# ScalarE issues the stores of h; the weights of the next expert are issued at the head of an item

## The chip, the cores and the metric

The kernel runs on one core of one Trainium2 chip. The metric is the device time of one execution in microseconds. Five engines work side by side: TensorE (PE; its weight loads are shown as PEld), VectorE (DVE), ScalarE (ACT), GpSimd (POOL) and SyncE (SP), which here only issues transfers and reads registers. Each engine works through its own instructions in order. A transfer is issued by one instruction and moved by 16 DMA engines. The three timed runs before the change took 784.21, 784.96 and 787.46 us; the median is 784.96 us.

## What is computed

Local attention with 32 global tokens for 8 batches of 8 heads (512 local queries, window 32, head size 64), then a mixture of experts over the 4352 resulting rows of 512. Each row goes to the one expert of eight with the largest logit:

```
for e in range(E):
    mask = expert_idx == e
    h = np.maximum(x[mask] @ w1[e], 0.0)
    out[mask] = gate_w[mask, None] * (h @ w2[e])
```

w1[e] is 512 x 1024 and w2[e] is 1024 x 512, all in float32. The change touches the second part only.

## The kernel before, in words

The attention part ends by scattering its rows, sorted by expert, into the DRAM tensor `xs`. The expert part then works on *items*: blocks of 128 rows that belong to one expert. 32 items always run; the rest, up to 48, stand in nested branches on the number of items (`rest`), and 36 run here. `item(w, pend)` writes one item's instructions; the order in it is the order on every engine, since it is written under a manual schedule.

Precision: a float32 product is made of three products in a faster form of float32. Each operand is split into a high part (a cast on ScalarE: `WH`, `xH`, `hH`) and a low part (operand less high part, on VectorE or GpSimd: `WL`, `xL`, `hL`). TensorE then sums high x high, high x low and low x high.

An item's path: its rows `xr` and gates `gt` come from `xs` (`load_x`, issued two items ahead: four transfers and one for gt). `up(0)` and `up(1)` are the two halves of x @ w1, twelve products each, into PSUM `g`. `relu` writes half of `h`. The half is then stored to DRAM (`put_h`, tile `hd`) and read back (`get_h`, tile `hq`), which does part of its transposition; VectorE turns it within blocks (`turn_h`, tile `hk`), and `split_h` makes hH and hL. In the item after, `down(0)` and `down(1)` are the two halves of h @ w2, and in the one after that `give` scales the result by the gate (line 173) and scatters it to the output. So TensorE's order in item w is up(0), up(1) of w, then down(0), down(1) of w-1.

Weights: an expert's 4096 x 2 columns per partition come through two stages, `st0[0]` and `st0[1]` (tile `stg`), one an item by turns. `load_w(w + 1)` fills the stage of the next item in two transfers of 1024 KB, each carried out only where a table says so; of one expert's four, most items carry out one or none. Every item casts its stage in eight parts, `w_part(0)` to `w_part(7)`: WH on ScalarE (line 1284), WL on VectorE, parts 0 and 4 on GpSimd (line 1286). They belong to the next expert, so no product of this item reads them. The parts of the first expert's weights (`first_parts`, line 1207 and 1209) are made from the stages before the first item.

Before the change, SP issues within item w: put_h 0, load_x(w + 2), get_h 0, put_h 1, load_w(w + 1), get_h 1. Each put_h waits for its relu. Register reads for the addresses and conditions (line 1217) stand ahead of load_x and load_w on SP. ScalarE's order is: line 173, parts 0 and 1, hH of the first half, parts 2 and 3, relu 0, parts 4 and 5, relu 1, hH of the second half, parts 6 and 7, xH of the next item.

Transfers issued by SP and ScalarE take turns at eight completion semaphores, shown as DMAHW0 to DMAHW7 in the order below; the next transfer of a lane waits until the one before it has landed.

Of the kernel before, what the change touches and what calls it, by code (L numbers as in the profile page):

```python
# [94 lines left out]
def _max_items(nt):  # L95
    return (nt - (NE - 1)) // P + 1 + 2 * (NE - 1)
# [11 lines left out]
def tile_kernel(ctx: ExitStack, tc: tile.TileContext, qk, va, emb, tau, wraw, cst, out):  # L108
    nc = tc.nc
# [3 lines left out]
    NI = _max_items(NT)  # L113
# [30 lines left out]
    def cols(st, lo, hi):  # L144

        r = lo // WRUN
        return st[:, r, lo - r * WRUN : hi - r * WRUN]
# [3 lines left out]
    def rows_of(x, gt, rows, turned=False):  # L151

        made = []
        for g in range(4):
            src = rows[:, g * P : (g + 1) * P].rearrange("(t i) n -> i t n", t=4)
            made.append(nc.sync.dma_start(x[32 * g : 32 * g + 32].rearrange("p (t n) -> p t n", n=P), src))
        src = rows[:, DM:ROW]
        made.append(nc.sync.dma_start(gt, src.rearrange("(i t) n -> t i n", t=4) if turned else src))
        return made
# [5 lines left out]
    def turn_blocks(xT, x):  # L165

        nc.vector.transpose(  # L167
            xT.rearrange("p (k t n) -> p t k n", k=4, t=4), x.rearrange("p (t k n) -> p t k n", t=4, k=4)
        )
# [99 lines left out]
    with ExitStack() as actx:  # L269
# [40 lines left out]
        parts = []  # L310
# [593 lines left out]
        for b in range(NB):  # L904
# [4 lines left out]
            for part in range(3):  # L909
                g = 4 * b + (2 + part // 2 if b else 4)  # L910
# [81 lines left out]
        for g in loads:  # L992
            n = len(loads[g])
# [209 lines left out]
    def first_parts(hf, c):  # L1203

        cs = slice(c * 1024, (c + 1) * 1024)
        src = cols(st0[hf], cs.start, cs.stop)
        nc.scalar.copy(WH[:, hf, cs], src)
        eng = nc.gpsimd if hf == 1 and c < 2 else nc.vector
        eng.tensor_tensor(WL[:, hf, cs], src, WH[:, hf, cs], ALU.subtract)
# [3 lines left out]
    def entry(eng, i, w, top):  # L1213

        if w < 2:
            return (EARLY * P + w * P, 2 + w, 0, 2 + w)[i]
        return eng.value_load(tab["tab"][w : w + 1, i : i + 1], min_val=0, max_val=top)

    def load_x(w):
        r = entry(nc.sync, 0, w, NE * CAP)  # L1220
        return rows_of(xrs[w % 2], gts[w % 5], xs[ds(r, P), :], True)

    def load_w(w):
        r = entry(nc.sync, 1, w, 2 * NE - 1)
        src = wraw[ds(r, 1), :, :].rearrange("a p (c n) -> p (a c) n", n=WRUN)
        for n in range(2):
            cs = slice(2 * n, 2 * n + 2)
            new = {} if w < 2 else {"cond": entry(nc.sync, 4 + n, w, 1)}
            nc.sync.dma_start(st0[w % 2][:, cs, :WRUN], src[:, cs, :], **new)

    def parts_of(tH, tL, x):
        nc.scalar.copy(tH, x)  # L1232
        nc.vector.tensor_tensor(tL, x, tH, ALU.subtract)  # L1233

    def flat(t):
        return t.rearrange("p c n -> p (c n)")
# [5 lines left out]
    def split_x(w):  # L1242
        parts_of(flat(xHs[w % 2]), flat(xLs[w % 2]), xk)
# [4 lines left out]
    hs = [h[:, :DM], h[:, DM:]]  # L1248

    def relu(nh, g):  # L1250
        nc.scalar.activation(
            hs[nh].rearrange("p (g k n) -> p k g n", g=4, k=4),
            g.rearrange("p (k g n) -> p k g n", k=4, g=4),
            AF.Relu,
        )

    def put_h(w, nh):
        hd = hds[w % 2][nh].rearrange("p n -> (p n)").rearrange("(g p n) -> p g n", g=4, p=P)
        nc.sync.dma_start(hd, hs[nh].rearrange("p (g n) -> p g n", g=4))

    def get_h(w, nh):
        nc.sync.dma_start(hqs[nh], hds[w % 2][nh])

    def turn_h(nh):
        turn_blocks(hk, hqs[nh])

    def split_h(nh):
        ks = slice(4 * nh, 4 * nh + 4)
        parts_of(flat(hH[:, ks, :]), flat(hL[:, ks, :]), hk)

    def item(w, pend):

        st, xH, xL = st0[w % 2], xHs[w % 2], xLs[w % 2]
        rp = entry(nc.tensor, 2, w, 1)
        ra = entry(nc.scalar, 3, w, 3)
        rv = entry(nc.vector, 3, w, 3)
        rg = entry(nc.gpsimd, 3, w, 3)
        reads = []
        made = []

        def w_part(c):
            cs = slice(c * 512, (c + 1) * 512)
            s3 = cols(st, cs.start, cs.stop).unsqueeze(1)
            made.append(nc.scalar.copy(WH[:, ds(ra, 1), cs], s3))  # L1284
            eng, r = (nc.gpsimd, rg) if c % 4 == 0 else (nc.vector, rv)
            made.append(eng.tensor_tensor(WL[:, ds(r, 1), cs], s3, WH[:, ds(r, 1), cs], ALU.subtract))  # L1286

        def product(o, a, W, col, start=False, stop=False):
            return nc.tensor.matmul(o.unsqueeze(1), a, W[:, ds(rp, 1), col : col + 512], start=start, stop=stop)  # L1289

        def up(nh):
            g = ps_1.tile([P, 512], F32, name="g1")
            for k in range(4):
                col = k * 1024 + nh * 512
                reads.append(product(g, xH[:, k, :], WH2, col, start=k == 0))
                reads.append(product(g, xH[:, k, :], WL2, col))
                reads.append(product(g, xL[:, k, :], WH2, col, stop=k == 3))
            return g

        out = {}  # L1300

        def down(nh):
            if nh == 0:
                out["g2"] = g2s[w % 2]
            g, ks, made = out["g2"], range(4 * nh, 4 * nh + 4), []
            for k in ks:
                made.append(product(g, hH[:, k, :], WH2, 4096 + k * 512, start=k == 0))
                made.append(product(g, hH[:, k, :], WL2, 4096 + k * 512))
            for k in ks:
                made.append(product(g, hL[:, k, :], WH2, 4096 + k * 512, stop=k == 7))  # L1310
            return made

        def done():
            give(gts[w % 5], out["g2"], obp.tile([P, DM + 1], F32, name="ob"))

        late = "down" in pend
        ga = up(0)
        if "done" in pend:
            pend["done"]()
        w_part(0)  # L1320
        if late:
            turn_h(0)
        w_part(1)
        if late:
            split_h(0)
        w_part(2)
        w_part(3)
        relu(0, ga)
        put_h(w, 0)
        if w + 2 < NI:  # L1330
            load_x(w + 2)
        gb = up(1)
        w_part(4)
        if late:
            turn_h(1)
        w_part(5)
        if late:
            reads.extend(pend["down"](0))
        relu(1, gb)
        get_h(w, 0)  # L1340
        put_h(w, 1)
        if w + 1 < NI:
            load_w(w + 1)
        if late:
            split_h(1)
        w_part(6)
        if 0 < w < NI - 1:
            turn_blocks(xk, xrs[(w + 1) % 2])
        w_part(7)
        if 0 < w < NI - 1:  # L1350
            split_x(w + 1)
        get_h(w, 1)
        if w in (8, NSURE - 1):
            nc.gpsimd.drain()
        if late:
            reads.extend(pend["down"](1))
        for m in made:
            for r in reads:
                tc.declare_no_dep(m.ins, r.ins, reason="the other slot")
                tc.declare_no_dep(r.ins, m.ins, reason="the other slot")  # L1360
            for o in last_made:
                if o.ins.engine != m.ins.engine:
                    tc.declare_no_dep(m.ins, o.ins, reason="another half")
        for i, m in enumerate(made):
            for o in made[: i // 2 * 2]:
                if o.ins.engine != m.ins.engine:
                    tc.declare_no_dep(m.ins, o.ins, reason="other columns")
        last_made[:] = made
        after = {"down": down, "next": done}
        if "next" in pend:  # L1370
            after["done"] = pend["next"]
        return after
# [10 lines left out]
    with tc.manual_schedule():  # L1383
        nc.vector.tensor_copy(runi, run[:1])
        for e in range(NE):
            fill_rest(e)
        load_x(0)
        load_x(1)
        tab["tab"], nitem = table()
        parts = [(hf, c) for hf in range(2) for c in range(4)]  # L1390
        for i, f in enumerate(block):
            if i == 9:
                x_parts(0)
            if i:
                f()
            for _ in range((3, 0, 1, 0, 0, 1, 0, 1, 0, 0, 0)[i]):
                first_parts(*parts.pop(0))
        x_parts(1)
        for hf, c in parts:
            first_parts(hf, c)  # L1400
        load_w(0)
        pend = {}
        for w in range(NSURE):
            pend = item(w, pend)
# [94 lines left out]
```

## Time and profile before

| | |
|---|---|
| median of three runs | 784.96 us (784.21 to 787.46) |
| the profiled execution | 784.63 us, span 782.80 us |
| mean granted clock of TensorE | 0.944 of full speed |
| busy over the span | PE 669.3, DVE 545.3, ACT 464.3, POOL 201.2 us |

The span runs from the first to the last instruction; the execution's own time is longer by what lies around it. Busy time is an average over parts with different limits: an engine that is busy 85% of the span can be idle in one place and the limit in another. So the trace is read by stretches and by waits. Register reads, waits and the issuing of transfers do not count as busy. "x2" in a line of the timeline means two instructions merged into one row, whose time is their sum; brackets show how long the engine sat idle before the row and what ended that. The row of a transfer on SPq is the time of its issue alone, not of the movement.

### The profile page before, as it was taken

How to read it: one execution, taken by the hardware profiler on the slowest of the kernel's cores; microseconds unless marked ns; L12 is line 12 of the kernel's file. 1: busy time of each engine (PE TensorE's matmuls, PEld its weight loads, DVE VectorE, ACT ScalarE, POOL GpSimd, SP SyncE). 2: the span in 40 equal slices, each digit the busy share in tenths (PEclk: the TensorE clock that was granted, in tenths of full speed). 3: DMA queues.
4: the chain of work that ended last, by engine and by line, in shares of the span. 5: the costliest groups of instructions: out<-in, count | busy, mean ns of one | idle time of the engine just before them, and what ended most of it. 6: DMA issues, size and time to landing. Idle time of an engine off the chain costs nothing. (4 is left out here: it accounts for less than half of the span.)

```text
span 782.8 us, 23722 instructions
## 1 busy us (share of the span) xinstructions
PE 669.3 (85%) x7425; PEld 505.0 (65%) x7425; DVE 545.3 (70%) x1642; ACT 464.3 (59%) x954; POOL 201.2 (26%) x246
## 2 busy tenths in 40 slices
PE   9888878798889967789999888968988878789994
PEld 4666666676665446567777666757666656567773
DVE  2667877887776755568889567657468666577892
ACT  4666776577672445557766456545456555566661
POOL 2001222222223522213333222322222222223231
PEclk9899999999998988889999999998999999989997
DMA  8888987888991874566545556556556567565441
GB/s 255 292 264 244 274 272 236 276 272 264 305 279 61 231 258 147 149 180 183 145 127 145 164 172 209 169 189 186 164 170 195 163 208 219 156 185 175 127 135 61
DMA packets 125596, 154.70 MB, mean 198 GB/s; under 512 B 15881, under 2 KB 81545, under 8 KB 125464
## 3 DMA queue, kind: packets, MB, share of 16 engines
q1 hardware_dynamic: 119704, 135.20, 58.3%
q0 software_dynamic: 5760, 17.87, 6.1%
q8 instruction: 68, 1.11, 0.6%
q14 instruction: 64, 0.52, 0.2%
HBM read 161.36 MB, written 40.94 MB: 258 GB/s over the span
## 5 line engine op out<-in xcount | busy, mean ns | idle before, releaser
L1286 DVE TENSOR_TENSOR WL<-stg,WH 128x512 f32 (+1 forms) x216 | 209.8, 973 | 104.8 <-ACT WH L1284 96.6
L1284 ACT CAST WH<-stg 128x512 f32 (+1 forms) x288 | 177.0, 618 | 113.6 <-DMA stg<-in_wraw_dram 109.0
L1289 PE MATMUL g<-WH,hH 128*128 (+1 forms) x288 | 127.6, 443 | 67.3 <-ACT hH L1232 67.1
L1286 POOL TENSOR_TENSOR WL<-stg,WH 128x512 f32 (+1 forms) x72 | 102.8, 1428 | 155.0 <-ACT WH L1284 128.3
L1289 PE MATMUL g<-WL,hH 128*128 (+1 forms) x288 | 123.4, 428 | 0.0
L1289 PEld LDWEIGHTS g<-WH,hH 128*128 128x128 f32 x288 | 59.6, 207 | 96.7 <-ACT hH L1232 79.8
L1289 PE MATMUL g<-WH,xH 128*128 (+1 forms) x288 | 114.2, 397 | 0.5 <-PE g L1289 0.5
L1289 PE MATMUL g<-WH,xL 128*128 (+1 forms) x288 | 114.2, 397 | 0.0
L1289 PE MATMUL g<-WL,xH 128*128 (+1 forms) x288 | 112.5, 391 | 0.0
L175 POOL DMA_INDIRECT out_dram<-ob x37 | 36.9, 997 | 210.7 <-DVE hk L167 81.5
L552 ACT ACTIVATE pb<-pb,nm 128x128 f32<-128x128 f32 x256 | 80.0, 395 | 12.6 <-DVE nm L535 12.1
L1289 PE MATMUL g<-WH,hL 128*128 (+1 forms) x288 | 82.8, 412 | 0.0
L167 DVE STREAM_TRANSPOSE hk<-hq 128x512 f32<-128x512 f32 x72 | 50.8, 705 | 30.7 <-DMA hq<-hd 30.7
L1289 PEld LDWEIGHTS g<-WH,hL 128*128 128x128 f32 x288 | 59.6, 207 | 13.8
L1289 PEld LDWEIGHTS g<-WL,hH 128*128 128x128 f32 x288 | 60.2, 209 | 12.2
L1289 PEld LDWEIGHTS g<-WH,xL 128*128 128x128 f32 x288 | 54.0, 188 | 16.1 <-DVE xL L1233 5.2
L1289 PEld LDWEIGHTS g<-WH,xH 128*128 128x128 f32 x288 | 54.1, 188 | 15.6 <-ACT xH L1232 5.3
L1289 PEld LDWEIGHTS g<-WL,xH 128*128 128x128 f32 x288 | 54.0, 188 | 11.8 <-DVE xk L167 0.2
L1232 ACT CAST hH<-hk 128x512 fp32r<-128x512 f32 x72 | 44.4, 616 | 26.5 <-DVE hk L167 25.0
L195 PE MATMUL s_ps<-raw 64*32 64x128 f32 (+1 forms) x1792 | 47.9, 284 | 11.0 <-issue 7.1
L195 PE MATMUL po<-vt,pT 128*32 128x65 f32 x2048 | 46.1, 231 | 12.2 <-issue 9.9
L837 POOL DMA_INDIRECT xs<-xt,si x32 | 32.6, 1019 | 76.6 <-PE s_ps L195 27.7
(201 smaller groups left out, 921.6 us busy)
## 6 DMA issues: line engine op xcount, KB each, us to landing
stg<-in_wraw_dram SPq DMA_DIRECT2D x74, 1024.0 KB
vt<-in_va_dram SPq DMA_DIRECT2D x96, 260.0 KB
hd<-h SPq DMA_DIRECT2D x72, 256.0 KB
hq<-hd SPq DMA_DIRECT2D x72, 256.0 KB
raw<-in_qk_dram SPq DMA_DIRECT2D x56, 304.0 KB
xr<-xs SPq DMA_DIRECT2D x152, 64.0 KB
vt<-in_va_dram SPq DMA_DIRECT2D x32, 130.0 KB
stg<-in_wraw_dram SPq DMA_DIRECT2D x16, 256.0 KB
```

The source lines that it names most:

```text
L167: nc.vector.transpose(xT.rearrange("p (k t n) -> p t k n", k=4, t=4), x.rearrange("p (t k n) -> p t k n", t=4, k=4))
L175: nc.gpsimd.indirect_dma_start(out=out[:, :], out_offset=bass.IndirectOffsetOnAxis(ap=ob[:, DM : DM + 1].bitcast(U32), axis=0), in_=ob[:, ...
L195: return counted(nc.tensor.matmul(out, lhsT, rhs, start=start, stop=stop), 4 if lhsT.dtype == F32 else 2)
L552: nc.scalar.activation(pb[:, cs], pb[:, cs], AF.Exp, bias=nm[:, n : n + 1], scale=-1.0)
L837: ins = nc.gpsimd.indirect_dma_start(out=xs[:, :], out_offset=bass.IndirectOffsetOnAxis(ap=st["si"][:, t : t + 1], axis=0), in_=get(t), in ...
L1232: nc.scalar.copy(tH, x)
L1284: made.append(nc.scalar.copy(WH[:, ds(ra, 1), cs], s3))
L1286: made.append(eng.tensor_tensor(WL[:, ds(r, 1), cs], s3, WH[:, ds(r, 1), cs], ALU.subtract))
L1289: return nc.tensor.matmul(o.unsqueeze(1), a, W[:, ds(rp, 1), col : col + 512], start=start, stop=stop)
```

## The change

put_h is issued by ScalarE, right behind its relu. In an item, load_w(w + 1) and load_x(w + 2) are issued first, the weights ahead of x, and both ahead of relu and put_h. Parts 3, 4 and 5 stand between the two relus. In the first item, which has no pending down product, relu and store come first, and the casts of w2's four parts, load_w(1) and all w_parts come behind them.

```diff
     def put_h(w, nh):
-        nc.sync.dma_start(hd, hs[nh].rearrange("p (g n) -> p g n", g=4))
+        nc.scalar.dma_start(hd, hs[nh].rearrange("p (g n) -> p g n", g=4))
...
         if "done" in pend:
             pend["done"]()
-        w_part(0)
+        if w and w + 1 < NI:
+            load_w(w + 1)
+        if w + 2 < NI:
+            load_x(w + 2)
         if late:
+            w_part(0)
             turn_h(0)
-        w_part(1)
-        if late:
+            w_part(1)
             split_h(0)
-        w_part(2)
-        w_part(3)
+            w_part(2)
         relu(0, ga)
         put_h(w, 0)
-        if w + 2 < NI:
-            load_x(w + 2)
         gb = up(1)
-        w_part(4)
         if late:
+            w_part(3)
+            w_part(4)
             turn_h(1)
-        w_part(5)
-        if late:
+            w_part(5)
             reads.extend(pend["down"](0))
+        else:
+            for _ in range(2):
+                first_parts(*parts.pop(0))
         relu(1, gb)
         get_h(w, 0)
         put_h(w, 1)
-        if w + 1 < NI:
-            load_w(w + 1)
         if late:
             split_h(1)
+        else:
+            while parts:
+                first_parts(*parts.pop(0))
+            load_w(w + 1)
+            for c in range(6):
+                w_part(c)
         w_part(6)
...
-            for _ in range((3, 0, 1, 0, 0, 1, 0, 1, 0, 0, 0)[i]):
+            for _ in range((3, 0, 1, 0, 0, 0, 0, 0, 0, 0, 0)[i]):
                 first_parts(*parts.pop(0))
         x_parts(1)
-        for hf, c in parts:
-            first_parts(hf, c)
```

On SP, from the second store of item 2 on, before (hd01 and hd00 are the halves of h in DRAM, stg0 and stg1 the stages; TENSOR_LOAD and ISA read and set registers):

```order
L1259 DMA hd01_59<-h_5768 128x4x128 [waits DMAHW5_49,Activation_49]
L1217 TENSOR_LOAD tab_5920
L1217 ISA x2
L1217 TENSOR_LOAD tab_5920
L1217 ISA x2
L1229 ISA
L1229 DMA stg1_90<-in_wraw_dram 128x2x1024 [waits Pool_49]
L1217 TENSOR_LOAD tab_5920
L1217 ISA x2
L1229 ISA
L1229 DMA stg1_90<-in_wraw_dram 128x2x1024 [waits DMAHW7_49,Pool_49]
L1262 DMA hq_5758<-hd01_59 128x512 [waits DMAHW5_49,DMAHW0_49,DVE_49]
```

The load of the weights for item 3 stands behind both stores of item 2, which wait for ScalarE, and ahead of the second read of h. On SP after the change, from the last transfer of x in item 3 on:

```order
L156 DMA xr1_5751<-xs_57 32x4x128 [waits DMAHW0_49]
L158 ISA
L158 DMA gt0_5752<-xs_57 128x1x2 [waits DMAHW1_49]
L1262 DMA hq_5758<-hd10_60 128x512 [waits DMAHW2_49,DVE_49]
L1262 DMA hq_5758<-hd11_61 128x512 [waits DMAHW4_49,DMAHW3_49,DVE_49]
L1217 TENSOR_LOAD tab_5920
L1217 ISA x2
L1217 TENSOR_LOAD tab_5920
L1217 ISA x2
L1229 ISA
L1229 DMA stg1_90<-in_wraw_dram 128x2x1024 [waits Activation_49,Pool_49]
```

The stores are gone from SP. The load behind the reads of item 3 is now item 4's own, for item 5, and no instruction of item 4 stands ahead of it. The waits on DMAHW1 and DMAHW3 are, by the count of transfers, those on the lanes of the two transfers of item 3's own load of weights.

On ScalarE within one item with a pending down product, before, from the first cast of hH to the second (h<-g is a relu, WH<-stg a part):

```order
L1232 CAST hH<-hk 128x512
L1284 ISA
L1284 COPY WH<-stg_90 128x512
L1284 ISA
L1284 COPY WH<-stg_90 128x512
L1251 ACTIVATE h<-g_6708 128x4x4x32
L1284 ISA
L1284 COPY WH<-stg_90 128x512
L1284 ISA
L1284 COPY WH<-stg_90 128x512
L1251 ACTIVATE h<-g_6754 128x4x4x32
L1232 CAST hH<-hk 128x512
```

Two parts stand before each relu. After the change, from the first relu to the second cast of hH:

```order
L1251 ACTIVATE h_5768<-g1_6210 128x4x4x32
L1259 DMA hd00_58<-h_5768 128x4x128
L1284 ISA
L1284 COPY WH_5748<-stg0_89 128x512
L1284 ISA
L1284 COPY WH_5748<-stg0_89 128x512
L1284 ISA
L1284 COPY WH_5748<-stg0_89 128x512
L1251 ACTIVATE h_5768<-g1_6283 128x4x4x32
L1259 DMA hd01_59<-h_5768 128x4x128
L1232 CAST hH_5766<-hk_5759 128x512
```

A store stands behind each relu, one part fewer stands before the first relu, and three stand between the two.

## Rows read from the trace of the kernel before

**Rows 1.** Stretches: us, busy time and count of each engine, granted clock, DMA share, GB/s
```profile
303.00:753.12 450.12, 396.26 (x1585) 306.21 (x1583) 314.17 (x429) 266.84 (x463) 126.21 (x99) 0.95 0.58 172
363.16:431.11 67.95, 67.93 (x289) 53.42 (x290) 60.57 (x79) 48.53 (x84) 24.08 (x18) 1.00 0.51 140
275.38:303.00 27.62, 18.63 (x73) 14.90 (x72) 17.52 (x21) 15.21 (x28) 7.70 (x5) 0.81 0.58 196
753.12:782.80 29.68, 19.20 (x72) 14.69 (x71) 13.85 (x20) 10.69 (x18) 5.79 (x5) 0.85 0.27 79
```

**Rows 2.** Waits, 303 to 753 us: engine and line, waited for; us, times, longest
```profile
ACT WH L1284 <- DMA stg<-in_wraw_dram: 99.1, 26, 8.2
...
PE g L1289 <- ACT hH L1232: 53.2, 27, 4.9
```

**Rows 3.** Timeline of one item with late weights: start, us, engine
```profile
561.86 0.38 SPq L1259 DMA_DIRECT2D hd<-h  x1
...
564.36 1.49 SPq L1229 DMA_DIRECT2D stg<-in_wraw_dram  x2
...
570.21 1.27 ACT L1284 CAST WH<-stg 128x512 f32 x2 [7.11 <-DMA stg<-in_wraw_dram]
...
572.05 0.50 PE L1289 MATMUL g<-WH,hH 128*128 x1 [3.79 <-ACT hH L1232]
...
573.08 0.60 ACT L1251 ACTIVATE h<-g 128x512 f32<-128x512 f32 x1
...
573.70 0.38 SPq L1259 DMA_DIRECT2D hd<-h  x1
```

**Rows 4.** Waits of SP over the whole span
```profile
SPq L1259 <- ACT h L1251: 150.2, 36, 7.7
```

**Rows 5.** Timeline of one undisturbed item
```profile
363.75 1.26 ACT L1284 CAST WH<-stg 128x512 f32 x2
...
365.64 0.39 PE L1289 MATMUL g<-WH,xL 128*128 x1
...
368.36 0.39 PE L1289 MATMUL g<-WH,xL 128*128 x1
...
368.78 0.60 ACT L1251 ACTIVATE h<-g 128x512 f32<-128x512 f32 x1 [0.42 <-PE g L1289]
...
370.71 0.62 ACT L1232 CAST hH<-hk 128x512 fp32r<-128x512 f32 x1 [1.33 <-DVE hk L167]
...
371.80 0.39 SPq L1259 DMA_DIRECT2D hd<-h  x1
...
373.20 0.65 DVE L1286 TENSOR_TENSOR WL<-stg,WH 128x512 f32 x1
...
374.31 0.09 SPq L1229 DMA_DIRECT2D stg<-in_wraw_dram  x1
```

**Rows 6.** Timeline of the first two items, SP and ScalarE
```profile
285.73 0.39 SPq L1259 DMA_DIRECT2D hd<-h  x1
286.17 1.11 SPq L1229 DMA_DIRECT2D stg<-in_wraw_dram  x2
...
289.03 0.34 SPq L1262 DMA_DIRECT2D hq<-hd  x1
...
293.50 0.62 ACT L1284 CAST WH<-stg 128x512 fp32r<-128x512 f32 x1 [9.90 <-DMA stg<-in_wraw_dram]
```

**Rows 7.** The line of put_h: shortest, median, longest issue in ns
```profile
L1259 SPq DMA_DIRECT2D hd<-h x72: 366/383/1327, 281.1 to 762.3; - x72
```

**Rows 8.** Timeline of TensorE, last product of the first item's first half
```profile
277.67 0.39 PE L1289 MATMUL g<-WH,xL 128*128 128x512 f32 x1
```

**Rows 9.** Tiles WH and WL, the first expert's parts: shortest, median, longest in ns
```profile
L1207 ACT CAST WH<-stg x8: 1037/1046/1053, 259.3 to 277.4; 128x1024 fp32r<-128x1024 f32 x8
...
L1209 DVE TENSOR_TENSOR WL<-stg,WH x6: 1202/1206/1224, 263.5 to 278.7; 128x1024 fp32r<-128x1024 f32 x6
```

**Rows 10.** Stretch of six items with weights, columns as in rows 1
```profile
616.42:706.76 90.34, 74.73 (x289) 56.60 (x290) 55.81 (x81) 48.54 (x85) 22.37 (x18) 0.94 0.61 185
```

## Prediction

> **What bounds the kernel now.** I read the stretch table first, then who waits for whom, then the timeline of one slow item and of one undisturbed item. The span splits in three: attention up to about 275 us, which the change leaves as it is; the first two items up to 303.00; and 33 items to 753.12, with a tail behind them [rows 1]. The 33 items take 450.12 us, 13.64 us each. But from 363.16 to 431.11 six items run in 67.95 us with TensorE busy 67.93 us of them at a granted clock of 1.00: 11.32 us an item [rows 1]. 33 such items would take 373.6 us; 76.6 us is lost over this stretch. 53.9 us of it is TensorE idle (450.12 - 396.26), the other 22.7 us is products that run longer at the mean clock of 0.95.
>
> Who is late? In this stretch TensorE waits 53.2 us for ScalarE's hH, 27 times, and ScalarE waits 99.1 us, 26 times, for staged weights [rows 2]. One such item shows how they hang together. SP puts out the second store of h at 561.86 and the weights only at 564.36; they are there for ScalarE at 570.21, 5.85 us later, and hH is queued behind their first two casts. TensorE's next product comes at 572.05 after 3.79 us of idle [rows 3]. So the weights are needed at the head of an item, and they are issued at about that same moment, because on SP they stand behind both stores of h, and these behind the two relus: SP waits 150.2 us for h, 36 times [rows 4].
>
> In an undisturbed item TensorE is the bound: twelve products from 365.64 to 368.36 are 0.227 us each, and 48 of them 10.9 us of the 11.32 [rows 5].
>
> **Part 1: the weights go out an item's length earlier.** When is the load issued? Take the undisturbed item whose second relu starts at 368.78 [rows 5]. Issued by ScalarE, its store goes out right behind that relu, about 369.5. The longest landing that I can bound is at the start, where a store begins at 285.73 with both halves of a load put behind it, and the read that needs it goes out at 289.03: 3.3 us [rows 6]. So the second read of h leaves SP at 373.2 at the latest. Now SP's next instructions are the register loads for the weights: before, from the end of the put at 372.19 to the slot of the load at 374.31, they take 2.1 us [rows 5]. That gives 375.7 at the latest. The stage that this load overwrites is read by the last subtraction of the item, on VectorE from 373.20 for 0.65 us [rows 5], so it is free in time. These weights are cast first in the item after next, 22.64 us (two items) after the cast at 363.75 [rows 5], that is 386.4. Slack: 10.7 us; a load takes 5.85 us [rows 3], and both halves of the early one 7.33 us, 286.17 to 293.50 [rows 6]. At least 3.4 us stays. So all 26 waits from 303 on should go: 76.6 us off the path.
>
> What is late next? Each load also delays what SP issues behind it. In the new order the read of gt carries a wait on the completion lane that the first half of the weights uses, and the second read of h one on the lane of the second half. A load that lands 5.85 us after its issue holds SP until about 381.6; the register loads and the four reads of x lie within that time, the store of the first half of h is just landing, and gt and both reads of h (about 0.4 us each) follow. The x read there is used an item later, the h after the next item's first products. I count nothing for this. Its cover is the rest of the item: should a load take over 10 us, the reads of h and then the next load slip.
>
> **Part 2: two stores an item on ScalarE.** Before, SP starts a store 0.02 us after its relu ends: relu 573.08 + 0.60, store 573.70 [rows 3]. The store occupies its queue 0.383 us in the median of 72, 1.327 us at the most [rows 7]. So one store holds ScalarE for about 0.4 us behind the relu's end, 0.5 us counting the 0.1 us by which ScalarE's instructions overlap. Two of them and the 8.1 us that ScalarE is busy in an undisturbed item (48.53 us over six [rows 1]) make 9.1 of 11.32 us. What counts is the cast of hH behind the second store, since TensorE waits for it. Sum: the first half's twelfth product begins at 365.64 and lasts as long as the row at 368.36, 0.39 us, to 366.03 [rows 5]; relu and store to 367.05; three casts (0.63 us each, by the pair of 1.26 [rows 5]) to 368.9; relu and store to 369.95. Before, this cast began at 370.71, held by VectorE's transpose, after 1.33 us of idle [rows 5]. So at 0.4 us a store I take a cost of nothing; VectorE's wait covers it. Bounds: at 1.33 us a store the cast moves to 371.8, 1.1 us late in every item, 36 us in all. On the other side the third cast comes after the first store now, VectorE and GpSimd meet at other moments, and the cast could come up to 0.4 us an item earlier (TensorE's floor is 10.9), 14 us in all. I take zero, since the median of 72 stores stands far below the 0.79 us a store (370.71 less 369.15, halved) from which the cover is used up.
>
> The Trainium skill (Perfetto Trace Analysis, "DMA Instruction — HWDGE (DVE, Sync)") says that the sequencers share the block that generates descriptors and that the time shown includes waiting for it. By that rule the first store, which falls into SP's four reads of x, could wait for some of them; no run here shows two issuers at once. With one read of x in front of a store the sum would not move, with all four it would be near the 36 us bound. The skill (DMA: Bandwidth & Descriptors, "Issuing engines are not separate DMA queues") also says that issuing from more engines saves only issue time; by that alone moving the stores would be worth nothing. The trace shows why order still counts here: SP's 150.2 us of waiting for h stands in front of the loads.
>
> **Part 3: the first item.** Relu and store come before the last four casts of w2 and the item's own casts. But the load of the second item's weights must wait for those four casts and their subtractions, which now come later: the first half's last product ends at 278.06 [rows 8], relu and store to 279.1, two casts of 1.05 us to 281.2, relu and store to 282.2, two casts to 284.3, and subtractions of 1.2 us each on VectorE behind them [rows 9], to about 286. Before, it left at 286.17 [rows 6]. Equal; I count zero, with 1.5 us to either side. The third item's weights now start behind the first item's subtractions, some ten of about 0.6 to 1.2 us after 286, so by 294; its casts are due after 303.00. The tail of 29.68 us [rows 1] has no load; I leave it.
>
> **The sum.** 303.00 + 33 x 11.32 + 29.68 = 706.2 us of span. The profiled execution took 784.63 us with a span of 782.80, so 1.8 us lie around it: 708.1 us. That execution is 0.3 us below the median of the three runs, which changes nothing: 708 us.
>
> **Rivals.**
> ScalarE too dear: its queue, not SP's, then holds hH. For it: a store of up to 1.33 us exists, the first store falls beside SP's four reads of x, and ScalarE never issued one in this program. Against: the median. Time: up to 1.1 us an item, 716 to 745 us.
> TensorE nearer its floor: the cast of hH comes earlier than VectorE allowed before. 33 x 10.95 in place of 33 x 11.32: 696 us.
> Transfers too slow: the same bytes in less time. Undisturbed items, without weights, show the DMA engines busy 0.51 [rows 1]. The densest stretch with weights, six items from 616.42 to 706.76, shows 0.61 [rows 10]: 9.2 us of DMA an item, which pressed into 11.32 us is 0.81. So loads would queue more than now; but even a load stretched to 10 us lands before the 386.4. If half of the 76.6 us stayed: 746 us.
> No effect: the load waits for something else, such as its stage. The stage's last reader, which is done at 373.85, speaks against it [rows 5]: 785 us.
> Slower: a store holds ScalarE until its data has landed, because the queue does not go on. The cast of hH then moves to 369.15 + 2c for a cost c per store, and the item grows by 2c - 1.56. From c = 1.94 us on, the item is over 13.64 and the kernel slower than now. At the 3.3 us that landing takes, an item is 16.4 us and the time 874 us. Against: SP's queue goes on after 0.38 us.
>
> **Chances.** Forecast, 703 to 717 us: 0.55. Nearer the floor, below 703: 0.15. ScalarE dear: 0.15. Half of the waits stay: 0.10. No effect: 0.02. Slower: 0.03. The range runs from 694, below the floor case, to 742, into the case of the half waits; what it leaves out is the last two cases, most of that one and the dear end of ScalarE's, under 2 in 10. The likeliest case's own range is the 703 to 717. Within 0.5% is what a measurement of this kernel can hardly tell from no change; faster 0.95, same 0.02, slower 0.03.
>
> **What would show it.** Part 1: ScalarE's wait for staged weights gone from 303 us on, the load issued within 2.5 us of the start of the item before the one that casts it, the granted clock 1.00 in that stretch. Part 2: stores on ScalarE's queue of about 0.4 us, ScalarE's idle before the second hH cast shorter but not gone. Part 3: TensorE's long wait before the first down products still there, up to 9 us, ending near 295. I am wrong if items with loads remain longer than those without, or if all items grow alike by more than 0.5 us.

## The result

The changed kernel takes 710.56 us (median of four runs, 708.21 to 718.29) against 785.3 us for the kernel before beside it: a ratio of 0.9062, 95% interval 0.8991 to 0.9134. In the later runs the same kernel was timed twice more against the kernel before, at 0.9101 (0.9049 to 0.9152) and 0.9060 (0.9021 to 0.9100). The forecast was 708 us.

The profiled execution took 710.51 us with a span of 708.70. Its stretches, with the columns and in the order of [rows 1] (first two items, the 33 items, the tail):

```profile
300.07:680.27 380.20, 368.92 (x1585) 295.69 (x1584) 309.98 (x429) 269.71 (x463) 124.31 (x99) 1.00 0.68 200
272.14:300.07 27.93, 19.00 (x73) 15.20 (x72) 19.35 (x21) 17.64 (x29) 12.80 (x7) 0.82 0.71 226
680.27:708.70 28.43, 18.46 (x72) 14.18 (x70) 13.27 (x19) 10.70 (x18) 5.58 (x5) 0.90 0.28 82
```

The gain lies in the 33 items: 450.12 us became 380.20. TensorE's idle time there fell from 53.9 to 11.3 us, and the granted clock rose from 0.95 to 1.00. The first two items took 27.62 us and now take 27.93. The rest of the difference stands ahead of them: they begin at 272.14 in place of 275.38. The code there is not quite as it was, since the casts of w2's four parts moved from there into the first item. But the kernel with only the stores moved, whose code there is that of before, begins them at 270.00, and among all the profiled executions shown below that point lies between 266.78 and 272.47. So I take this for scatter and not for an effect.

Who waits for whom, from 300 to 680 us, in answer to [rows 2]:

```profile
DVE hk L167 <- DMA hq<-hd: 36.5, 20, 4.1
ACT hH L1232 <- DVE hk L167: 30.2, 31, 3.3
...
PE g L1289 <- ACT hH L1232: 11.2, 14, 2.0
```

ScalarE's wait for staged weights, 99.1 us before, is not in this list at all. A new one leads to what TensorE still waits for: VectorE waits 36.5 us for h read back from DRAM. SP's own waits, in answer to [rows 4]:

```profile
SPq L1262 <- DMA hd<-h: 108.3, 61, 4.9
...
SPq L158 <- DMA stg<-in_wraw_dram: 16.7, 12, 3.2
```

SP used to wait for the relu. Now it waits for the store to land, so that it may read it back. The line of put_h, in answer to [rows 7]; the store now stands on ScalarE's queue:

```profile
L1259 ACTq DMA_DIRECT2D hd<-h x72: 366/371/414, 275.5 to 686.6; - x72
```

One item of the new kernel, 10.88 us long, for comparison with [rows 5]:

```profile
401.16 0.69 ACT L173 ACTIVATE ob<-g,gt 128x512 f32<-128x512 f32 x1 [0.84 <-PE g L1289]
...
401.96 1.47 SPq L1229 DMA_DIRECT2D stg<-in_wraw_dram  x2
...
403.96 0.59 ACT L1251 ACTIVATE h<-g 128x512 f32<-128x512 f32 x1
404.23 2.10 SPq L156 DMA_DIRECT2D xr<-xs  x4
...
404.57 0.37 ACTq L1259 DMA_DIRECT2D hd<-h  x1
...
405.08 1.93 ACT L1284 CAST WH<-stg 128x512 f32 x3 [0.53 <-ACT h L1251]
...
405.54 1.48 DVE L1286 TENSOR_TENSOR WL<-stg,WH 128x512 f32 x2
...
406.49 1.68 POOL L1286 TENSOR_TENSOR WL<-stg,WH 128x512 f32 x1 [2.03 <-issue]
...
407.94 0.62 ACT L1232 CAST hH<-hk 128x512 fp32r<-128x512 f32 x1 [0.44 <-DVE hk L167]
...
410.14 1.14 SPq L1262 DMA_DIRECT2D hq<-hd  x2
```

The weights leave 0.8 us into the item before the one that casts them. A store starts 0.02 us after its relu ends and keeps ScalarE from its next cast for 0.53 us. The second hH is cast 6.78 us after the line 173 that opens the item; before, it was 7.55 us (363.16 to 370.71). And the first store, issued at 404.57, is read back only at 410.14: 5.6 us, with a load in flight.

A long item shows what is left. It starts with line 173 at 480.64; its first rows lie in the item before:

```profile
471.23 2.25 SPq L1229 DMA_DIRECT2D stg<-in_wraw_dram  x2
...
473.51 0.37 ACTq L1259 DMA_DIRECT2D hd<-h  x1
...
476.83 0.65 SPq L158 DMA_DIRECT2D gt<-xs  x1
...
481.73 1.96 SPq L1262 DMA_DIRECT2D hq<-hd  x2
...
485.06 0.71 DVE L167 STREAM_TRANSPOSE hk<-hq 128x512 f32<-128x512 f32 x1 [4.09 <-DMA hq<-hd]
...
485.81 0.62 ACT L1232 CAST hH<-hk 128x512 fp32r<-128x512 f32 x1 [3.32 <-DVE hk L167]
```

Both transfers of weights are carried out here, 2 MB; 2.28 us behind them comes the store, and it is 8.2 us from the store to the read that needs it. SP was through with gt at 477.48 and had nothing else to do. The transpose comes 4 us late, hH behind it, and relu 0 and the next store behind hH. In a stretch without loads of weights the same two steps look so:

```profile
370.99 0.37 ACTq L1259 DMA_DIRECT2D hd<-h  x1
...
373.70 4.16 SPq L1262 DMA_DIRECT2D hq<-hd  x2
```

That is 2.7 us.

### The profile page after: what moved, and what is told of

The parts are those of the page before. It is cut to its first block, busy times and chain, and to the rows that moved or that the text cites. A ratio compares the mean times of both kernels' runs of the same rounds, so it can differ in the third digit from the quotient of the medians.

```text
span 708.7 us, 23788 instructions
## 1 busy us (share of the span) xinstructions
PE 635.8 (90%) x7425; PEld 490.2 (69%) x7425; DVE 541.1 (76%) x1642; ACT 467.4 (66%) x954; POOL 199.7 (28%) x246
## 5 line engine op out<-in xcount | busy, mean ns | idle before, releaser
L1286 DVE TENSOR_TENSOR WL<-stg,WH 128x512 f32 (+1 forms) x216 | 204.1, 947 | 25.4 <-ACT WH L1284 22.7
L1289 PE MATMUL g<-WH,hH 128*128 (+1 forms) x288 | 117.5, 408 | 25.0 <-ACT hH L1232 24.9
L1289 PE MATMUL g<-WL,hH 128*128 (+1 forms) x288 | 115.4, 401 | 0.0
L1289 PEld LDWEIGHTS g<-WH,hH 128*128 128x128 f32 x288 | 55.6, 193 | 44.9 <-ACT hH L1232 28.8
L167 DVE STREAM_TRANSPOSE hk<-hq 128x512 f32<-128x512 f32 x72 | 50.8, 706 | 36.7 <-DMA hq<-hd 36.5
L1289 PE MATMUL g<-WH,hL 128*128 (+1 forms) x288 | 78.0, 393 | 0.0
L1289 PEld LDWEIGHTS g<-WL,hH 128*128 128x128 f32 x288 | 55.9, 194 | 11.1
L1289 PEld LDWEIGHTS g<-WH,hL 128*128 128x128 f32 x288 | 55.1, 191 | 11.8
L1233 DVE TENSOR_TENSOR hL<-hk,hH 128x512 fp32r<-128x512 f32 x72 | 49.3, 685 | 7.0 <-ACT hH L1232 5.6
```

What stands on the lines that cost most here:

```text
L167: nc.vector.transpose(xT.rearrange("p (k t n) -> p t k n", k=4, t=4), x.rearrange("p (t k n) -> p t k n", t=4, k=4))
```

## Experiments

Below, "the 33 items" is the time from the third item's line 173 to the 36th's, and "the changed kernel" has 380.2, 379.4 and 375.6 us there in three profiled executions, the last two beside the experiments.

**The order alone.** Stores back on SP.

```diff
-        nc.scalar.dma_start(hd, hs[nh]...
+        nc.sync.dma_start(hd, hs[nh]...
```

> The changed kernel with the stores of h put back on SP; the weights and x stay at the head of the item. Theory (the two parts need each other): SP now has to do in turn, for every item, two register reads (2.1 us), the weights' slots (1.2), a register read and x and gt (4.0), the first store (0.4), its landing (2.7 us at the least), a read (0.4), the second store (0.4), its landing (2.7), a read (0.4): about 14.2 us an item against the 11.32 of TensorE. So every item, with weights or without, grows to about 14 us and the kernel takes 780 to 810 us. Rival (the place of the weights alone brings the gain): within 10 us of the changed kernel, 700 to 720 us.

Measured: 799.24 us (two runs), 1.030 of the kernel before (1.020 to 1.041). The theory held. SP's queue in one item, in order of time:

```profile
418.45 0.39 SPq L1259 DMA_DIRECT2D hd<-h  x1
420.81 0.35 SPq L1262 DMA_DIRECT2D hq<-hd  x1
421.25 1.08 SPq L1259 DMA_DIRECT2D hd<-h  x1
425.40 0.33 SPq L1262 DMA_DIRECT2D hq<-hd  x1
427.50 1.86 SPq L1229 DMA_DIRECT2D stg<-in_wraw_dram  x2
430.18 1.88 SPq L156 DMA_DIRECT2D xr<-xs  x4
432.26 0.64 SPq L158 DMA_DIRECT2D gt<-xs  x1
433.01 0.41 SPq L1259 DMA_DIRECT2D hd<-h  x1
```

From one first store to the next it is 14.56 us: a store, its landing, the second store, its landing, then weights, x and gt, all in one queue. TensorE needs 10.88. The early weights by themselves make the kernel slower.

**The stores alone.** The kernel before with the one line of put_h changed.

```diff
-        nc.sync.dma_start(hd, hs[nh]...
+        nc.scalar.dma_start(hd, hs[nh]...
```

> The kernel before with the two stores on ScalarE and nothing else moved: the weights still follow the first read of h. Theory (order matters, the stores only clear the way): a load now goes out some 2.2 us earlier in an item, as it no longer waits for the second relu, but still only 2 to 3 us before its casts; about half of ScalarE's wait for staged weights stays, 735 to 760 us. Rival (SP's 150 us of waiting for h was the cause by itself): 705 to 720 us. Rival (the stores' engine is without effect): 780 to 790 us.

Measured: 744.63 us, 0.9598 (0.9542 to 0.9653). The theory held.

```profile
294.12:713.85 419.73, 381.26 (x1585) 300.00 (x1584) 311.99 (x428) 268.84 (x462) 121.39 (x99) 0.98 0.60 183
```

The 33 items take 419.73 us, 30 us less than before; ScalarE still waits for staged weights:

```profile
ACT WH L1284 <- DMA stg<-in_wraw_dram: 58.7, 23, 4.9
```

Putting the weights first then takes off another 39.5 us (419.73 to 380.20). The kernel before was itself faster beside this run than beside the changed kernel (777.1 and 785.3 us), so the ratios are the safer measure: from 0.960 to between 0.906 and 0.910, some 39 to 42 us. So neither part does the work of the other, and the order needs the stores out of its way. Items that wait for nothing take 10.88 us here as well, with the old order of casts: this gain comes with the stores on ScalarE, not with the third cast's new place.

**No weights in flight.** From the third item on.

```diff
+            if w >= 2:
+                continue
             nc.sync.dma_start(st0[w % 2][:, cs, :WRUN], src[:, cs, :], **new)
```

> The changed kernel without the transfers of weights from the third item on; their casts stay, so the later experts are computed with wrong weights. Theory (what is still lost in the 33 items, 380 us against 33 x 10.9 = 360, comes in part from loads that delay the round trip of h, in part from the order on VectorE and GpSimd, as in five items without loads that took 11.25 us each): long items gone, all near 11.25, 698 to 704 us. Rival (all of it comes from the loads): items of 10.9 us, 688 to 694 us. Rival (loads have no part in it): 708 to 712 us, with items of 12 to 15 us left.

Measured: 688.5 us (two runs), 0.8875 (0.8807 to 0.8942).

```profile
298.17:658.17 360.00, 359.60 (x1585) 297.09 (x1584) 312.64 (x429) 267.46 (x462) 130.49 (x99) 1.00 0.51 144
```

32 of the 33 items take 10.88 to 11.02 us and one 11.60, and TensorE is never idle but for 0.4 us. My theory named 11.25 us for an item and failed; the first rival held. So what the 33 items of the changed kernel still lose against these 360.00 us, 15.6 to 20.2 us over its three profiled executions, comes with the transfers of weights; their register reads are kept here.

**Half the bytes.** The same transfers with half their columns, so that the other half of the later experts' weights is missing.

```diff
+            m = WRUN if w < 2 else WRUN // 2
-            nc.sync.dma_start(st0[w % 2][:, cs, :WRUN], src[:, cs, :], **new)
+            nc.sync.dma_start(st0[w % 2][:, cs, :m], src[:, cs, :m], **new)
```

> The changed kernel with each transfer of weights from the third item on cut to half its columns (the other half is left as it was, so later experts have wrong weights); the number of transfers, register reads and lanes stays. Theory (the bytes in flight delay the store): a large part of the 20 us that all 33 items lost against 10.88 each goes, 5 to 10 us of it left, 692 to 699 us where the changed kernel takes 710. Rival (each transfer costs by its presence, by a wait or a lane): no more than 4 us below the changed kernel.

Measured: 694.1 us (two runs), 0.8926 (0.8884 to 0.8968), where the changed kernel beside it took 705.15.

```profile
299.65:663.00 363.35, 361.64 (x1585) 296.32 (x1584) 317.53 (x430) 267.93 (x462) 129.73 (x99) 1.00 0.61 176
```

Against the kernel without loads 3.4 us of the loss are left, where the changed kernel beside it has 15.6; that is less than I expected. The number of transfers, packets and waits is the same here, so it is bytes in flight that delay the round trip, not the presence of a transfer. A shorter load also ends the waits on its lane earlier; that these are not the cause is read from the changed kernel's own trace, under the next run.

**x ahead of the weights.**

```diff
-        if w and w + 1 < NI:
-            load_w(w + 1)
         if w + 2 < NI:
             load_x(w + 2)
+        if w and w + 1 < NI:
+            load_w(w + 1)
```

> The changed kernel with x ahead of the weights at the head of the item. gt is then issued before the load, so no wait of gt on the load's lane stands before the reads of h; but the load goes out some 4 us later in the item, beside the first store. Theory (a load in flight delays the landing of the store, and the lane of gt does not matter): items with weights get longer by 0 to 1.5 us, 0 to 25 us above the changed kernel. Rival (SP held by gt on the load's lane makes the long items): 8 to 20 us below it.

Measured: 721.13 us, 0.9251 (0.9199 to 0.9303), 11 us above the changed kernel beside it. The theory's number held, but not its mechanism. In the profiled execution (729.11 us, its longest) most first stores land as early as without a load; what comes late is the read:

```profile
313.85 0.37 ACTq L1259 DMA_DIRECT2D hd<-h  x1
...
317.91 1.77 SPq L1229 DMA_DIRECT2D stg<-in_wraw_dram  x2
319.79 0.88 SPq L1262 DMA_DIRECT2D hq<-hd  x2
```

By its semaphore this store has landed 2.7 us after its issue, yet the read goes out after 5.9 us, behind the register reads and the load, and then moves beside that load; the item after it takes 15.14 us. So the load only took another place ahead of the read, and this run can't tell whether gt's wait on the load's lane matters. The changed kernel's own trace can. In 21 of its 33 items weights move between the issue of the first store and its landing; in 20 of them gt had been issued before the store had landed, in the other one 0.03 us after it, and in all of them the read went out within 0.15 us of the landing. So gt's wait is not what makes items long. That weights ahead of x is the faster of these two orders is shown by the times.

**Weights spread over the item.** First half at the head, second half and x behind the first read of h.

```diff
-            load_w(w + 1)
-        if w + 2 < NI:
+            load_w(w + 1, (0,))
+        if not w:
             load_x(w + 2)
...
         get_h(w, 0)
+        if w and w + 1 < NI:
+            load_w(w + 1, (1,))
+        if w and w + 2 < NI:
+            load_x(w + 2)
         put_h(w, 1)
```

> The changed kernel with only the first half of the weights at the head of the item; the second half and x are issued behind the first read of h, so that they do not lie beside the first store and its read. In the changed kernel the items after a second-half load are the long ones (11.5 to 15.5 us, the first read of h lands late), those after a first-half load are 10.9 to 11.1. Theory (a load in flight delays the store's landing and thereby the next item): these items fall to about 11.2 us, 697 to 703 us. Rival (the long items come from SP waiting on the weights' lane with gt): the wait is still there for the first half, but gt is behind the read of h now, so as well 697 to 703; the trace then tells by the time from store to read. Rival (half of the weights come too late this way): items with a second half wait for staged weights, 710 to 725 us.

Measured: 710.77 us, 0.9161 (0.9111 to 0.9211), the 33 items 381.86 us. No gain: the theory's number failed. The time falls into the range of the third rival, 710 to 725 us, but not by its mechanism, since ScalarE waits only 3.5 us for staged weights. The wait moved:

```profile
DVE hk L167 <- DMA hq<-hd: 40.3, 30, 2.9
...
ACT WH L1284 <- DMA stg<-in_wraw_dram: 3.5, 7, 1.3
```

VectorE waits more often and less long. A first half still goes out just ahead of the first store, and SP's queue, in order, now reads the second half of h later.

**All weights behind the first read of h.** Registers read ahead of it, x behind, first hH ahead of parts 0 to 2.

```diff
-        if w and w + 1 < NI:
-            load_w(w + 1)
-        if w + 2 < NI:
+        regs = regs_w(w + 1) if w and w + 1 < NI else None
+        if not w:
             load_x(w + 2)
...
         get_h(w, 0)
+        if regs:
+            load_w(w + 1, regs)
+        if w and w + 2 < NI:
+            load_x(w + 2)
         put_h(w, 1)
```

> The changed kernel with the weights issued right behind the first read of h (their registers are read ahead of it), x behind them, and the first cast of hH ahead of parts 0 to 2. So the first store and its read have the DMA engines to themselves; the second store, needed some 5 us later in the next item, meets the load. Theory (the store's landing beside a load is what makes items long; without it items take 10.88 us): 8 to 18 us below the changed kernel, turn of the first half no longer waiting for its read. Rival (the load then lands too late for parts 0 to 2): ScalarE's wait for staged weights returns in 10 or more items, 0 to 30 us above the changed kernel.

Measured: 718.05 us, 0.9193 (0.9129 to 0.9257), 8 us above the changed kernel beside it.

```profile
ACT WH L1288 <- DMA stg<-in_wraw_dram: 8.4, 9, 3.5
DVE hk L167 <- DMA hq<-hd: 6.9, 5, 2.5
```

(The lines are four further down here.) The wait for h did go, from 37.0 us in the changed kernel beside it to 6.9, as the theory said; but staged weights come late nine times (8.4 us), the two items whose weights come in both halves at once take 16.00 and 15.38 us, and the items between settle at 11.1 instead of 10.88. The 33 items take 384.78 us, 379.4 in the changed kernel beside it. By the medians the rival held on the sum, though the two intervals just overlap (0.9129 to 0.9257 against 0.9049 to 0.9152).

**The turn behind the store.** Turn and split of the first half of h behind the first relu and store.

```diff
-            turn_h(0)
             w_part(1)
-            split_h(0)
...
         put_h(w, 0)
...
+            turn_h(0)
+            split_h(0)
             w_part(3)
             w_part(4)
             turn_h(1)
-            w_part(5)
...
             split_h(1)
+            w_part(5)
```

> The changed kernel with the turn and split of the first half of h moved behind the first relu and store (parts 0 to 2, relu, store, turn, hH, parts 3 and 4, relu, store, hH of the second half, part 5). Theory (a load in flight delays the first store and thereby the read that ScalarE's whole queue stands behind): the read has some 3 us more, and a late read no longer delays relu and store of the next item, so items of 12 to 15 us fall to 11 to 11.5; 6 to 14 us below the changed kernel. Rival (the loss is DMA throughput itself, the engines being busy up to 0.93 of an item): no gain, within 3 us. Rival (hH of the second half comes too late now, in every item): 5 to 20 us above it.

Measured: 729.63 us, 0.9392 (0.9354 to 0.9430), 24 us above the changed kernel beside it (705.15), more than the third rival's 20.

```profile
300.54:698.40 397.86, 382.59 (x1585) 290.20 (x1583) 299.57 (x428) 273.88 (x462) 119.49 (x99) 1.00 0.63 190
```

No item but one is above 12.6 us any more, and VectorE's wait for h is no longer among the waits that matter. But most items take 11.95 us, since the turns and splits of both halves now follow one another between ScalarE and VectorE: from 300 to 690 us ScalarE waits 56.5 us for hk, 64 times, and VectorE 48.5 us for hH. A cure for a loss of 16 to 20 us, at a price of 1.07 us on every item.

**The first item as before.** On top of the change, and on top of the kernel with the late turn.

```diff
-            for _ in range((3, 0, 1, 0, 0, 0, 0, 0, 0, 0, 0)[i]):
+            for _ in range((3, 0, 1, 0, 0, 1, 0, 1, 0, 0, 0)[i]):
                 first_parts(*parts.pop(0))
         x_parts(1)
+        for hf, c in parts:
+            first_parts(hf, c)
...
+        else:
+            for c in range(4):
+                w_part(c)
         relu(0, ga)
...
```

> The changed kernel with the first item put back: the casts of w2's parts ahead of the items, the item's own casts around the relus, the second item's weights as before; only the store stays on ScalarE. Theory (the first item's new order is worth nothing, since TensorE's long wait there ends with the weights of the second item, and these leave at the same moment): within 2 us of the changed kernel. In the kernel with only the stores moved, that wait was 4.81 us in place of 8.9 and the two items took 24.1 in place of 27.9 us; a rival is therefore that the new order of the first item costs 3 to 4 us, and this kernel is 3 to 4 us faster. Rival (it brings what the trace shows at the head, 3.2 us earlier): 3 us slower.

> The same with the first item's order of before as well. Theory (the new first item cost 3.2 us by the trace, 24.6 in place of 27.8 us for the first two items): 3 us below the kernel with the late turn alone, 9 to 17 us below the changed kernel. Rival (the 3 us is the difference of two profiled executions only): the same as with the late turn alone, and 27 to 28 us for the first two items.

Measured: 706.63 us, 0.9087 (0.9039 to 0.9134), beside 709.94 us for the changed kernel; and 725.75 us, 0.9354 (0.9313 to 0.9394), beside 729.63. Each is 3 to 4 us faster than its neighbour in the median, and the intervals overlap in both pairs, so the timing does not settle it. The profiles agree in both: the first two items take 24.59 us in place of 27.79, and 26.06 in place of 29.32.

```profile
266.78:291.37 24.59, 19.00 (x73) 15.22 (x72) 17.27 (x21) 15.66 (x28) 6.25 (x5) 0.86 0.87 302
```

What holds hH in the second item of the changed kernel:

```profile
284.74 5.82 DVE L1286 TENSOR_TENSOR WL<-stg,WH 128x512 fp32r<-128x512 f32 x6
...
286.94 1.14 ACT L1284 CAST WH<-stg 128x512 fp32r<-128x512 f32 x2 [1.91 <-DMA stg<-in_wraw_dram]
...
290.48 0.70 DVE L167 STREAM_TRANSPOSE hk<-hq 128x512 f32<-128x512 f32 x1
...
291.21 0.62 ACT L1232 CAST hH<-hk 128x512 fp32r<-128x512 f32 x1 [3.13 <-DVE hk L167]
```

The weights are there at 286.94, 14.8 us after the stretch begins (in the kernel with the first item undone 14.7: 281.50). But hH waits 3.13 us more for VectorE, which does the first item's subtractions, moved behind everything, before it turns h. The rival that the new first item costs 3 to 4 us held in the profiles. No kernel tried that still loads all the weights is faster than the changed one beyond its interval.

**Repeats.** The changed kernel unaltered, as the measure for its neighbours:

> The changed kernel itself once more, as the measure for the three that run beside it on this chip. Every theory: 0.90 to 0.915 of the kernel before.

> The changed kernel once more, as the measure on this chip. Every theory: 0.90 to 0.915 of the kernel before.

Measured: 709.94 us, 0.9101, and 705.15 us, 0.9060, as told above.

## Why the prediction was right, and where it was not

**The weights an item earlier: right.** The load goes out 0.8 us into the item (I had allowed 2.5), no cast waits for staged weights from 300 us on, and with the idle time the low clock went too: 1.00 over the stretch. TensorE's busy time there fell by 27.3 us (396.26 to 368.92), the 22.7 us of slowed products that I had worked out and 4.6 us more. That the load needs the stores off SP was not a step of mine; the two single changes showed it, at 0.960 and 1.030.

**The stores on ScalarE: the cost right, the gain missed.** 0.371 us a store in the median, 0.414 at the most; ScalarE's wait before the second hH is 0.44 us in the item shown, shorter than 1.33 and not gone, as I said. But I took zero from a range that reached 14 us of gain, and the gain is the end of that range: 10.88 for 11.32 us an item, 14.5 us over 33. By the rows, VectorE's two subtractions ahead of the second turn take 1.48 us in the item shown, and GpSimd's part starts 0.95 us after the first of them; the change of order between these two is what I had named as unknown. In the undisturbed item of before the pair took 2.38 us, with GpSimd's part starting 0.16 us after it; in the kernel with only the stores moved it takes 1.48 again, with GpSimd's part 0.96 us after its start:

```profile
367.68 2.38 DVE L1286 TENSOR_TENSOR WL<-stg,WH 128x512 f32 x2
367.84 1.67 POOL L1286 TENSOR_TENSOR WL<-stg,WH 128x512 f32 x1 [1.25 <-issue]
```

```profile
374.14 1.48 DVE L1286 TENSOR_TENSOR WL<-stg,WH 128x512 f32 x2
375.10 1.69 POOL L1286 TENSOR_TENSOR WL<-stg,WH 128x512 f32 x1 [2.04 <-issue]
```

So the store alone brings the new timing: it comes ahead of ScalarE's cast for GpSimd's part and puts that part off. The pair is 0.90 us shorter, and 0.89 us is also what ScalarE's wait before the second hH lost (1.33 to 0.44). That the overlap with GpSimd made the old pair longer is still my reading of the rows; no experiment moved GpSimd alone.

The rule of the Trainium skill on the shared descriptor block (Perfetto Trace Analysis, "DMA Instruction — HWDGE (DVE, Sync)") can now be put beside a run. The store at 404.57 falls among SP's four reads of x from 404.23 on and takes 0.37 us, like the others; the longest of all 72 took 0.414. If stores waited for the block here, it was for under 0.05 us.

**What is late next: this step failed.** I bounded a store's landing by 3.3 us, from one store near a load, and counted nothing for what the load delays. But in that row the load stood behind the store (286.17 after 285.73), and in the new order it stands ahead. Measured from store to read, it is 2.7 us in the item shown without a load, 5.6 us with 1 MB and 8.2 us with 2 MB; over the 33 items 5.0 to 8.2 us in the 21 whose first store met a load, 2.5 to 4.6 us in the 12 others. The read then comes too late for the next item's first turn: after all five reads that came over 7 us behind their store, the next item took 12.1 to 15.5 us. Without loads the 33 items take 360.0 us and with half the bytes 363.35, so the term that I set to zero is 16 to 20 us. By the sign that I had set myself, items with loads that remain longer than those without, I was wrong here. I looked for the delay in SP's queue (gt on the load's lane); it lies in the transfer of the store itself.

The trace also lists every packet that the DMA engines moved, with its queue, and these show where the time goes. In the 12 items without a load the store's first packet moves 0.9 to 1.2 us after its issue. In 20 of the 21 with one it moves after 2.2 to 4.1 us, when of a load of 1 MB more than 85% of the packets had begun, and of the two loads of 2 MB two thirds; in the other item the load's packets began behind the store's. With half the bytes the first packet is never later than 2.2 us. A packet of the store takes 27 ns in the median with a load and without. So the store mostly stands in line behind the load, though it comes from another queue.

**The sum was closer than its terms.** 33 x 11.32 = 373.6 against 380.2: a missed gain of 14.5 us and a missed loss of 20 us partly cancel. That the forecast of 708 us lies so near the 710.56 measured is in part luck. With the scatter at the head (-3.2) and the tail (-1.2) the span came to 708.7 against 706.2.

**The first item: right in the number, wrong in the reason.** 27.93 us against 27.62, and TensorE's long wait is 8.93 us, where it was 8.99 before. But the stores alone shorten these two items to 24.12 us, and the new order gives it back, through VectorE and no longer through the weights.

**The rivals.** ScalarE too dear and the store that holds ScalarE until it lands: excluded by 0.37 us on its queue. TensorE nearer its floor: this came true for the items that nothing disturbs, 10.88 us, but not for the sum. Transfers too slow: this is the one that came true in part, 20 of the 76.6 us where I had priced 38, and by a path I had not named.

**Open.** After a disturbed item, items without any load alternate between 11.0 and 11.6 us for a while before they fall back to 10.88; between 344.91 and 401.16 that is 11.25 us on average. Without loads it happened once in 33 items. What holds this state up I have not settled. Nor is it shown why the DMA engines let a store on another queue stand behind a load: that it stands there, and that the bytes matter, is shown, the rule by which they choose is not.

## What to carry to other kernels

An in-order transfer queue is a chain like any other: write down what one round of it costs, landings included, and compare that with the engine that should be the bound; here the same new order gave 0.906 with the stores on another queue and 1.030 without. When a large load is moved away from a wait, ask which small transfer with a short deadline it now flies beside, and take that one's landing time from rows with such a load ahead of it, not behind it. And where two unknown terms are set to zero, a good sum says little about either.

## What the runs showed of the hardware

A 256 KB store to DRAM on ScalarE's queue, from its issue to the read that waits for it, in the first stores of the changed kernel's 33 items: 2.5 to 4.6 us with no weights moving, 5.0 to 8.2 us with 1 to 2 MB issued on SP's queue up to 2.6 us before it (in one item just behind it). Its first packet moved after 0.9 to 1.2 us without weights, and after 2.2 to 4.1 us in 20 of the 21 items with them. An issue on ScalarE held up its next cast by 0.53 us after the relu, for 0.37 us of issue. Without loads of weights TensorE ran 32 of 33 items within 0.14 us of 10.88 at a clock of 1.00; the other took 11.60.
